# The residual's product, the last copy and the store at the tail of a one-token decode layer

## The chip, the cores and the metric

The kernel runs on one core of one Trainium2 chip. Its time is the device time of one execution in microseconds; lower is better. The kernel before took 191.78 us, the median of 3 runs (191.37 to 191.93).

## The reference, cut to what matters

One token of width 512 goes through an attention block with a cached history of 16384 positions (32 query heads, 8 key and value heads of width 128), and then through a block of four matrices. The two residual sums at the end are what the change touches.

```python
x = A_x
h = x + _A_ref(_layernorm(x), A_k_cache, A_v_cache, A_wq, A_wo)
h2 = h + _B_ref(_layernorm(h), B_w1, B_w2, B_w3, B_w4)

def _B_ref(x, w1, w2, w3, w4):
    h = _gelu(_layernorm(x) @ w1)
    ...                      # four blocks of h, each shifted along the token axis
    x1 = x + hs              # one token only: every shift leaves zeros, so hs is 0
    h2 = _gelu(_layernorm(x1) @ w3) @ w4
    return x1 + h2
```

With one token the shifted part is zero, so the kernel never loads `w1` and `w2`. What is left after the attention is: normalise h twice, multiply by `w3` (512 to 1792), gelu, multiply by `w4` (1792 to 512), and add h and the once normalised h. The output is 512 numbers in bf16, 1024 bytes.

## The kernel before, in words

All large loads go through SP's queue, and their transfers run one after the other: the query matrix, then keys and values of four pairs of heads, then `wo`, `w3` and `w4`. VectorE transposes the keys, TensorE makes scores and weighted values, and ScalarE takes the exponentials. After the last pair follows the tail: the attention's output through `wo` (line 728), the sum with x and its statistics (lines 482 to 533), the product with `w3` (line 746), gelu on ScalarE (line 758), a transpose on VectorE (line 762), the product with `w4` (line 772), a copy out of PSUM (line 777) and the store (line 778).

The product with `w4` takes 1792 rows as 14 parts of 128, m = 0 to 13. `W4` cuts its load into four pieces: parts 0 to 4, 5 to 9, 10 to 12, and 13. A part's matmuls wait for its piece. For each m there are four matmuls, o = 0 to 3: each has 32 columns of weights (`hcol[:, m, :]`, the same column 32 times) and writes 32 partitions of one PSUM bank, so that partitions 32o to 32o + 31 hold the o-th quarter of the result, 32 times over.

The residual h plus normalised h is `xsum`, [128, 128] in fp32, made by GpSimd (line 755); it has the same four quarters on its partitions. Ahead of part 10 one fp32 matmul with the identity (line 768, 128 columns of weights, the full array) adds it into the same bank. Then comes a mark, `pe(None)`: there the program sets a branch that is never taken back. VectorE has such a mark, `dve(None)`, behind its last transpose; before the change nothing of the kernel follows it there.

The order of work on each engine is the order in which the program calls `P.op`. Waits come from its lists of who wrote and read each key. One rule bears on the change: a `bank` key makes an operation wait for the latest operation of every other engine that named the same bank, whether it reads or writes:

```python
for k in bank:
    for e, o in self.users.get(k, {}).items():
        if e != eng:
            need(o, False)
```

Of the kernel before, what the change touches and what calls it, by code (L numbers as in the profile page):

```python
# [7 lines left out]
BF16 = mybir.dt.bfloat16  # L8
I32 = mybir.dt.int32
ALU = mybir.AluOpType  # L10
ACTF = mybir.ActivationFunctionType
# [316 lines left out]
NHC = FM // 128  # L328
WO = ((0, 12), (12, 24), (24, 30), (30, 32))
VP = 2  # L330
W3 = ((0, 2), (2, 3), (3, 4))
W4 = ((0, 5), (5, 10), (10, 13), (13, 14))
PAIRS = HKV // 2
RPARTS = 9
QPAD = 4 * 7
# [6 lines left out]
def bass_sequential_preLN__gqa_block_cached__mixer_s_mlp__decode_kernel(  # L342
# [13 lines left out]
    with ExitStack() as ctx:  # L356
        sb = lambda name, shape, dt: ctx.enter_context(nc.sbuf_tensor(name, shape, dt))
        ps = lambda name, shape, dt: ctx.enter_context(nc.psum_tensor(name, shape, dt))
        P = Program(nc, ctx)
# [15 lines left out]
        ident_f = sb("ident_f", [128, 128], FP32)  # L375
# [12 lines left out]
        xn = sb("xn", [128, NCH], BF16)  # L388
        qcol = sb("qcol", [128, 4, PAIRS * REP, 32], FP32)
        qb = sb("qb", [128, 4, PAIRS, QW], BF16)  # L390
        qn = sb("qn", [128, 4, QW], BF16)
# [19 lines left out]
        xsum = sb("xsum", [128, 128], FP32)  # L411
        hg = sb("hg", [128, FQ], BF16)
        hT = sb("hT", [128, NCH, 32], FP32)
        hcol = sb("hcol", [128, NHC, 32], BF16)
        fin = sb("fin", [128, 128], BF16)
        kb_all = sb("kb", [128, 256 * DH], BF16)
        kb = [kb_all[:, i * 128 * DH:(i + 1) * 128 * DH] for i in range(2)]
        vb = sb("vb", [128, 256 * DH], BF16)
# [3 lines left out]
        w4_sb = kb[1][:, NCH * FM:2 * NCH * FM].rearrange("p (m c) -> p m c", m=NHC)  # L422
# [6 lines left out]
        m_ps, n_ps = mn_ps[:, 0:256], mn_ps[:, 256:512]  # L429


        def load(name, dst, src, key, by="SP", also=()):
            P.op(by, lambda e: e.dma_start(dst, src), w=[key, *also], dma=name)

        def pair_rows(src, j):
            return src[0, 2 * j:2 * j + 2].rearrange("g (u t) d -> (g u) (t d)", u=64)
# [6 lines left out]
        def load_values(j):  # L443
            n = 256 // VP * DH
            if j < PAIRS - 1:
                load("v", vb[:, :], pair_rows(A_v_cache, j), ("v", 0),
# [11 lines left out]
        def dve(fn, r=(), w=(), bank=()):  # L458
            return P.op("DVE", fn, r, w, bank)

        def act(fn, r=(), w=(), bank=()):
            return P.op("ACT", fn, r, w, bank)
# [4 lines left out]
        def pe(fn, r=(), w=(), bank=(), also=()):  # L467

            return P.op("PE", fn, r, w, bank, also=also)

        def piece(cuts, m):
            return [lo <= m < hi for lo, hi in cuts].index(True)
# [48 lines left out]
        def inverse_root(i, n, by):  # L521
# [7 lines left out]
            for k in range(3):  # L529
# [22 lines left out]
            r=["ident", "x4"], w=["quarter"])  # L552
        pe(lambda e: e.matmul(O_ps[0][:, 0:128], quarter[:, :, :].rearrange("p q u -> p (q u)"), x4[:, :],
                              start=True, stop=True), r=["quarter"], w=[("O", 0)], bank=[("O", 0)])
# [9 lines left out]
            r=["ident_f"], w=["row32"])  # L564
        dve(lambda e: e.tensor_reduce(maskdd[:, :], ident_f[:, :].rearrange("p (n d) -> p d n", d=4), AX.X, ALU.add),
            r=["ident_f"], w=["maskdd"])
# [6 lines left out]
        for z, m, key, mk in ((zo, rowgh, "zo", "rowgh"), (zd, maskgh, "zd", "maskgh")):  # L573
# [5 lines left out]
            r=["hT", (("st", 0), 0), (("st", 0), 6)] + [("v", x) for x in range(VP)], w=["xn"])  # L579
# [3 lines left out]
        for i, key in enumerate(keys):  # L583
            P.part("query", i)
            for k in range(NCH):
                pe(lambda e, k=k: e.matmul(row[:, bass.ds(P.b, 512)], copies(xn[:, k:k + 1], 128),  # L586
                                           wq_k[:, k, bass.ds(P.c, REP * DH)], start=(k == 0), stop=(k == NCH - 1)),
                   r=["xn"], also=[("v", x) for x in range(VP)], w=["n" if key == "mn" else key], bank=[key])
        P.part()
        for g in range(2):  # L590
            half = banks[64 * g:64 * g + 64, PAIRS * g:PAIRS * g + PAIRS, :].rearrange("p j c -> p (j c)")
            for b in range(2):
                dve(lambda e, g=g, b=b, half=half: e.transpose(  # L593
                    qcol[64 * g:64 * g + 64, 2 * b:2 * b + 2, :, :].rearrange("p e m u -> p (e m u)"),
                    half.rearrange("p (m b i e) -> p b e m i", b=2, i=32, e=2)[:, b, :, :, :]),
                    r=["n" if x == "mn" else x for x in keys[PAIRS * g:PAIRS * g + PAIRS]], w=["qcol"],
                    bank=keys[PAIRS * g:PAIRS * g + PAIRS])
        for a in range(4):
# [118 lines left out]
        w4_in = B_w4.rearrange("(p m) c -> p m c", p=128)  # L717
        for n, (lo, hi) in enumerate(W4):
            load(f"w4{n}", w4_sb[:, lo:hi, :], w4_in[:, lo:hi, :], ("r", 1, len(W3) + n))
# [3 lines left out]
            r=["o_m"], w=["o_f"])  # L723
        dve(lambda e: e.tensor_copy(o_b[:, :], o_f[:, :]), r=["o_f", ("r", 0, 0)], w=["o_b"])  # L724

        for r_ in range(32):
            q = r_ % 4
            pe(lambda e, r_=r_, q=q: e.matmul(O_ps[0][32 * q:32 * q + 32, :], copies(o_b[:, r_:r_ + 1], 32),  # L728
                                              wo_sb[:, r_ * D:(r_ + 1) * D], start=(r_ < 4), stop=(r_ >= 28)),
               r=["o_b"] + [("r", 0, n) for n in (piece(WO, r_),) if n], w=[("O", 0)], bank=[("O", 0)])  # L730
        h_ps, hkey = banks[:, 6, :], "spare0"
        dve(lambda e: e.tensor_copy(osum[:, :], O_ps[0][:, :]), r=[("O", 0)], w=["osum"], bank=[("O", 0)])
        for q in range(4):
            pe(lambda e, q=q: e.matmul(h_ps[32 * q:32 * q + 32, 0:128], copies(row32[:, 0:1], 32),
                                       osum[:, q * 128:(q + 1) * 128], start=True, stop=True),
               r=["osum", "row32"], w=[hkey], bank=[hkey])
# [4 lines left out]
            r=["hT", (S, 0)] + [("r", 1, 0)], w=["hc"])  # L741


        for k in range(NCH):
            for q in range(4):
                pe(lambda e, k=k, q=q: e.matmul(s_ps[32 * q:32 * q + 32, 0, 0:FQ], hc[:, k, :],
                                                w3_sb[:, k, q * FQ:(q + 1) * FQ], start=(k == 0), stop=(k == NCH - 1)),
                   r=["hc"] + [("r", 1, n) for n in (piece(W3, k),) if n], w=[("s", 0)], bank=[("s", 0)])
# [5 lines left out]
            r=["hr", (S, 0), (S, 6)], w=["xs"])  # L754
# [9 lines left out]
                hg[:, :].rearrange("p (i m) -> p m i", m=NHC)[:, lo:hi, :]), r=[("hg", n)], w=[("hcol", n)])  # L764
        dve(None)
        for m in range(NHC):
            if m == W4[-2][0]:
                pe(lambda e: e.matmul(n_ps[:, 0:128], ident_f[:, :], xsum[:, :], start=False, stop=False,
                                      skip_group_check=True), r=["ident_f", "xsum"], w=["n"], bank=["mn"])
                pe(None)  # L770
            for o in range(4):
                pe(lambda e, m=m, o=o: e.matmul(  # L772
                    n_ps[32 * o:32 * o + 32, 0:128], hcol[:, m, :], w4_sb[:, m, o * 128:(o + 1) * 128],
                    start=(m == 0), stop=(m == NHC - 1),
                    skip_group_check=True),
                   r=[("hcol", 2 * m // NHC), ("r", 1, len(W3) + piece(W4, m))], w=["n"], bank=["mn"])
        act(lambda e: e.activation(fin[:, :], n_ps[:, 0:128], ACTF.Identity), r=["n"], w=["fin"], bank=["mn"])
        P.op("SP", lambda e: e.dma_start(out[0, 0:1, :].rearrange("o (q j) -> (o q) j", q=4), fin[0:128:32, :]),
             r=["fin"], w=["out"], dma="out")
        P.op("SP", lambda e: e.nop(), r=["out"])  # L780
        P.emit()

# [29 lines left out]
```

## Time and profile before

| | us |
|---|---|
| median of the runs shown | 191.78 |
| the three runs | 191.93, 191.78, 191.37 |
| profiled execution: span from first to last instruction | 190.4 |
| the median less that span | 1.4 |
| TensorE busy in the span | 118.6 |
| VectorE busy in the span | 118.2 |
| ScalarE busy in the span | 9.3 |

Of the profiled execution the page gives the span alone. Its own time is the span and what lies ahead of and behind it; taken at the median, that is 190.4 and 1.4. The transfers moved 79.20 MB at a mean of 416 GB/s over the span. A timeline row gives the start, the length, the engine, the line, the operation, the tiles and shapes, how many instructions are merged in it, and in brackets the idle time before it with what ended it. PE is TensorE's matmuls, PEld its weight loads, DVE VectorE, ACT ScalarE, POOL GpSimd and SPq the queue of SP.

### The profile page before, as it was taken

How to read it: one execution, taken by the hardware profiler on the slowest of the kernel's cores; microseconds unless marked ns; L12 is line 12 of the kernel's file. 1: busy time of each engine (PE TensorE's matmuls, PEld its weight loads, DVE VectorE, ACT ScalarE, POOL GpSimd, SP SyncE). 2: the span in 40 equal slices, each digit the busy share in tenths (PEclk: the TensorE clock that was granted, in tenths of full speed). 3: DMA queues.
4: the chain of work that ended last, by engine and by line, in shares of the span. 5: the costliest groups of instructions: out<-in, count | busy, mean ns of one | idle time of the engine just before them, and what ended most of it. 6: DMA issues, size and time to landing. Idle time of an engine off the chain costs nothing.

```text
span 190.4 us, 2182 instructions
## 1 busy us (share of the span) xinstructions
PE 118.6 (62%) x695; PEld 46.1 (24%) x695; DVE 118.2 (62%) x155; ACT 9.3 (5%) x16; POOL 7.3 (4%) x16
## 2 busy tenths in 40 slices
PE   0119709996195599940944989508449995294644
PEld 0103203442031143310311433203113332031212
DVE  6740799995504989845049989350479895504370
ACT  3000000000200000011000000020000000500020
POOL 7100000000000000000000000000000000000060
PEclk9999985899958579995585899975979999758855
DMA  6999999999999999997999999979999999989991
GB/s 227 434 441 441 441 441 441 441 441 441 413 441 406 420 523 441 441 441 330 441 441 441 523 441 413 441 324 420 413 441 441 441 441 441 441 367 421 409 411 51
DMA packets 3619, 79.20 MB, mean 416 GB/s; under 512 B 416, under 2 KB 544, under 8 KB 1568
## 3 DMA queue, kind: packets, MB, share of 16 engines
q1 hardware_dynamic: 3608, 79.17, 97.2%
q8 instruction: 1, 0.02, 0.0%
q14 instruction: 2, 0.02, 0.0%
q10 hardware_dynamic: 8, 0.00, 0.0%
HBM read 79.17 MB, written 0.00 MB: 416 GB/s over the span
## 4 chain that ended last, share of the span: by engine, by line
PE 39%; DMA 37%; DVE 16%; issue 4%; ACT 2%; ACTq 0%; SPq 0%; DVEq 0%
DMA kb<-in_A_k_cache_dram 31%; PE banks L626 22%; PE banks L662 6%; DMA vb<-in_A_wq_dram 6%; DVE kt L609 6%; PE banks L586 5%; DVE pt L651 3%; PE banks L728 2%; DVE mx L636 1%; ACT p_sb L647 1%; PE banks L620 1%; DVE od L681 1%; PE banks L772 1%; DVE qcol L593 1%; PE banks L639 1%
## 5 line engine op out<-in xcount | busy, mean ns | idle before, releaser
L609 DVE STREAM_TRANSPOSE kt<-kb 128x2048 int32<-128x2048 int32 (+1 forms) x37 | 71.3, 1987 | 4.3 <-DMA kb<-in_A_k_cache_dram 2.8
L626 PE MATMUL banks<-kt,qn 128*128 x256 | 68.7, 414 | 0.5
L626 PEld LDWEIGHTS banks<-kt,qn 128*128 x256 | 26.2, 102 | 41.4 <-issue 24.6
L662 PE MATMUL banks<-vb,pt 128*32 128x512 bf16 x256 | 24.4, 565 | 2.8 <-POOLq L448 2.8
L678 DVE TENSOR_SCALAR od<-banks,rowc 128x128 f32<-128x128 f32 x4 | 1.4, 350 | 26.3 <-PE banks L662 26.3
L620 PE MATMUL banks<-qn 128*128 128x512 bf16 x8 | 4.0, 495 | 17.3 <-DVE kt L609 17.1
L651 DVE STREAM_TRANSPOSE pt<-p_sb 64x1024 bf16<-64x1024 bf16 x8 | 9.9, 1239 | 5.4 <-ACT p_sb L647 5.3
L662 PEld LDWEIGHTS banks<-vb,pt 128*32 128x32 bf16 x256 | 9.0, 136 | 16.4 <-issue 12.4
L586 PE MATMUL banks<-vb,xn 128*128 x32 | 8.9, 446 | 6.1 <-DVE xn L577 6.1
L669 PE MATMUL banks<-acc,zd 128*32 128x1 f32 x8 | 1.1, 202 | 17.7 <-DVE pt L651 17.7
L647 ACT ACTIVATE p_sb<-banks,bias 128x1024 bf16<-128x1024 f32 x4 | 4.5, 1113 | 155.4 <-DVE nmh L643 155.4
L636 DVE TENSOR_REDUCE mx<-banks 128x1 f32<-128x1024 f32 x4 | 4.9, 1224 | 8.1 <-PE banks L626 8.1
L593 DVE STREAM_TRANSPOSE qcol<-banks 64x1024 f32<-64x1024 f32 x4 | 4.8, 1226 | 6.9 <-PE banks L586 6.9
L528 POOL TENSOR_SCALAR st<-st 128x1 f32<-128x1 f32 x1 | 0.2, 241 | 176.1 <-DVE st L513 176.1
L586 PEld LDWEIGHTS banks<-vb,xn 128*128 128x128 bf16 x32 | 3.6, 112 | 11.0 <-issue 8.5
L639 PE MATMUL banks<-mxd,mean 128*128 128x128 f32 x8 | 2.0, 326 | 6.6 <-DVE mxd L637 6.6
L620 PEld LDWEIGHTS banks<-qn 128*128 128x128 bf16 x8 | 0.8, 100 | 20.2 <-issue 20.0
L684 PE MATMUL banks<-od,zo 128*32 128x128 f32 x8 | 1.6, 285 | 6.5 <-DVE od L681 6.5
L669 PEld LDWEIGHTS banks<-acc,zd 128*32 128x32 f32 x8 | 0.7, 140 | 18.4 <-DVE pt L651 18.4
L681 DVE SCALAR_TENSOR_TENSOR od<-banks,rowc,od 128x128 f32<-128x128 f32 x12 | 4.2, 351 | 0.4
L550 DVE CAST ident<-ident_f 4x4 bf16<-4x4 f32 x1 | 3.8, 3848 | 0.6 <-POOL ident_f L545 0.6
L728 PE MATMUL banks<-kb,o_b 128*32 128x512 bf16 x32 | 3.5, 583 | 1.1 <-DVE o_b L724 1.1
(78 smaller groups left out, 44.6 us busy)
## 6 DMA issues: line engine op xcount, KB each, us to landing
kb<-in_A_k_cache_dram SPq DMA_DIRECT2D x8, 4096.0 KB, 29.7
vb<-in_A_v_cache_dram SPq DMA_DIRECT2D x2, 4096.0 KB, 29.2
vb<-in_A_wq_dram SPq DMA_DIRECT2D x1, 4096.0 KB, 12.3
kb<-in_A_wo_dram SPq DMA_DIRECT2D x2, 1536.0 KB, 25.4
kb<-in_B_w_dram SPq DMA_DIRECT2D x2, 640.0 KB, 25.4
kb<-in_B_w_dram SPq DMA_DIRECT2D x1, 896.0 KB, 22.4
kb<-in_B_w_dram SPq DMA_DIRECT2D x2, 448.0 KB, 23.4
kb<-in_A_wo_dram SPq DMA_DIRECT2D x1, 768.0 KB, 28.5
```

What stands on the lines that cost most here:

```text
L586: pe(lambda e, k=k: e.matmul(row[:, bass.ds(P.b, 512)], copies(xn[:, k:k + 1], 128), wq_k[:, k, bass.ds(P.c, REP * DH)], start=(k == 0), s ...
L593: dve(lambda e, g=g, b=b, half=half: e.transpose(qcol[64 * g:64 * g + 64, 2 * b:2 * b + 2, :, :].rearrange("p e m u -> p (e m u)"), half.r ...
L609: P.op("DVE", lambda e, view=view: e.transpose(view(kt), view(kb[y])), r=[("r", y, i) for i in range(RPARTS)], w=[("kt", t + i) for i in r ...
L620: pe(lambda e: e.matmul(row[:, bass.ds(P.y, 512)], copies(none, 128), copies(none, 512), start=True, stop=False, skip_group_check=True), r ...
L626: pe(lambda e, n=n: e.matmul(row[:, bass.ds(P.y, 512)], qn[:, n, bass.ds(P.q, 128)], key_piece(P.k, n), start=False, stop=(n == 3), skip_g ...
L636: dve(lambda e: e.tensor_reduce(mx[:, :], s_all, AX.X, ALU.max), r=[("s", 0), ("s", 1)], w=["mx"], **both)
L639: pe(lambda e: e.matmul(m_ps[:, 0:128], mean4[:, :], mxd[:, :], start=True, stop=True), r=["mxd", "mean4"], w=["m"], bank=["mn"])
L647: act(lambda e: e.activation(p_sb[:, :], s_all, ACTF.Exp, bias=bias[:, 0:1], scale=float(SCALE), accum_out=acc[:, :]), r=[("s", 0), ("s", ...
L651: dve(lambda e, g=g: e.transpose(pt[64 * g:64 * g + 64, :, :, g, :], p_sb[64 * g:64 * g + 64, :]), r=["p"], w=["pt"])
L662: pe(lambda e, l=l, ct=ct, ch=ch: e.matmul(O_ps[0][32 * ct:32 * ct + 32, :], pt[:, l, ch, :, :].rearrange("p g u -> p (g u)"), tiles[:, l ...
L681: dve(lambda e, block=block, c=c: e.scalar_tensor_tensor(od[:, :], block, rowc[:, c:c + 1], od[:, :], ALU.mult, ALU.add), r=[key, "rowc", ...
L728: pe(lambda e, r_=r_, q=q: e.matmul(O_ps[0][32 * q:32 * q + 32, :], copies(o_b[:, r_:r_ + 1], 32), wo_sb[:, r_ * D:(r_ + 1) * D], start=(r ...
```

## The change

Three edits in the last 20 lines:

- The residual's product moves from ahead of part 10 to ahead of part 7 (`NHC // 2`, the first part of the second half), and becomes four matmuls of 32 columns of weights instead of one of 128. The mark `pe(None)` stays ahead of part 10.
- The four quarters are written to the partitions in the order 0, 2, 1, 3 (`BLOCK`). So partition 31 and partition 32, which are neighbours, hold quarters 0 and 2 of the result in the lower half of the bank, and the upper half of the bank holds quarters 1 and 3. ScalarE copies partitions 0 to 63 into the first 128 columns of `fin`, VectorE copies partitions 64 to 127 into the second 128. Partition 31 of `fin` is then the first half of the output, partition 32 the second.
- The store takes these two rows of 512 bytes instead of four rows of 256 bytes, and waits for both copies.

```diff
+BLOCK = (0, 2, 1, 3)
...
-        fin = sb("fin", [128, 128], BF16)
+        fin = sb("fin", [64, 256], BF16)
...
         for m in range(NHC):
+            if m == NHC // 2:
+                for o in range(4):
+                    pe(lambda e, o=o: e.matmul(
+                        n_ps[32 * o:32 * o + 32, 0:128], ident_f[:, 32 * BLOCK[o]:32 * BLOCK[o] + 32], xsum[:, :],
+                        start=False, stop=False, skip_group_check=True),
+                       r=["ident_f", "xsum"], w=["n"], bank=["mn"])
             if m == W4[-2][0]:
-                pe(lambda e: e.matmul(n_ps[:, 0:128], ident_f[:, :], xsum[:, :], start=False, stop=False,
-                                      skip_group_check=True), r=["ident_f", "xsum"], w=["n"], bank=["mn"])
                 pe(None)
             for o in range(4):
                 pe(lambda e, m=m, o=o: e.matmul(
-                    n_ps[32 * o:32 * o + 32, 0:128], hcol[:, m, :], w4_sb[:, m, o * 128:(o + 1) * 128],
+                    n_ps[32 * o:32 * o + 32, 0:128], hcol[:, m, :], w4_sb[:, m, BLOCK[o] * 128:(BLOCK[o] + 1) * 128],
...
-        act(lambda e: e.activation(fin[:, :], n_ps[:, 0:128], ACTF.Identity), r=["n"], w=["fin"], bank=["mn"])
-        P.op("SP", lambda e: e.dma_start(out[0, 0:1, :].rearrange("o (q j) -> (o q) j", q=4), fin[0:128:32, :]),
-             r=["fin"], w=["out"], dma="out")
+        act(lambda e: e.activation(fin[:, 0:128], n_ps[0:64, 0:128], ACTF.Identity),
+            r=["n"], w=[("fin", 0)], bank=["mn"])
+        dve(lambda e: e.tensor_copy(fin[:, 128:256], n_ps[64:128, 0:128]), r=["n"], w=[("fin", 1)], bank=["mn"])
+        P.op("SP", lambda e: e.dma_start(out[0, 0:1, :].rearrange("o (q j) -> (o q) j", q=2), fin[31:33, :]),
+             r=[("fin", 0), ("fin", 1)], w=["out"], dma="out")
```

## The prediction

> **What bounds the kernel now.** I read the page first, then the tail alone: its timeline, its chain of waits, its stretches by window, and the groups by line. The page:
>
> ```profile
> span 190.4 us, 2182 instructions
> PEclk9999985899958579995585899975979999758855
> DMA  6999999999999999997999999979999999989991
> ```
>
> The transfers are busy in every slice but the first and the last, so until the last weights have landed the kernel runs at their pace. Nothing in the change touches that. What counts is the last slices: there the transfers stop, and TensorE's granted clock is half.
>
> ```profile
> 184.41 1.04 DVE L762 STREAM_TRANSPOSE hcol<-hg 128x224 bf16<-128x224 bf16 x2 [0.61 <-ACT hg L758]
> 185.22 0.45 POOL L755 TENSOR_TENSOR xsum<-hr,xs 128x128 f32<-128x128 f32 x1
> 185.76 0.46 PEld L772 LDWEIGHTS banks<-kb,hcol 128*32 128x32 bf16 x20 [0.26 <-DMA kb<-in_B_w_dram]
> 186.16 0.33 PE L772 MATMUL banks<-kb,hcol 128*32 128x128 bf16 x4
> 186.41 0.50 PEld L768 LDWEIGHTS banks<-xsum,ident_f 128*128 128x128 f32 x2 [0.20 <-issue]
> 186.42 0.80 PE L768 MATMUL banks<-xsum,ident_f 128*128 128x128 f32 x2
> 187.14 0.62 PE L772 MATMUL banks<-kb,hcol 128*32 128x128 bf16 x16
> 187.81 0.28 ACT L777 ACTIVATE fin<-banks 128x128 bf16<-128x128 f32 x1 [3.08 <-PE banks L772]
> 188.12 0.63 SPq L778 DMA_DIRECT2D out_dram<-fin  x1
> ```
>
> This is the tail's timeline. Part 5 of the last matrix starts at 185.76, when its piece has landed; part 9's four matmuls are the row at 186.16. The residual's product then holds TensorE from 186.41, and part 10 starts at 187.14. After the last matmul come a copy of 0.28 and the store's issue. The store's wait is in the view of who waits for whom on SP's queue:
>
> ```profile
> SPq L780 <- DMA out_dram<-fin: 1.6, 1, 1.6
> ```
>
> So the store takes 0.63 of issue and 1.6 of waiting, from 188.12 to the span's end at 190.4: longer than TensorE takes from part 5 to its last matmul, 185.76 to 187.76. Three terms can move: when TensorE ends, how long the copies take, and the store.
>
> **The product moved.** First, how early could part 10 start at all? Its piece is the 384 KB load, part 13's the 128 KB one:
>
> ```profile
> 165.63 3.16 SPq L433 DMA_DIRECT2D kb<-in_B_w_dram  x1
> 168.83 0.43 SPq L433 DMA_DIRECT2D kb<-in_B_w_dram  x1
> kb<-in_B_w_dram SPq DMA_DIRECT2D x1, 384.0 KB, 21.1
> kb<-in_B_w_dram SPq DMA_DIRECT2D x1, 128.0 KB, 18.2
> ```
>
> Issue plus time to landing: 165.63 + 21.1 = 186.73 and 168.83 + 18.2 = 187.03. A wait hands over in about 0.03 (worked out below), so part 10 can't start before 186.76. Now it starts at 187.14: the product's place costs 0.38 at most, and that is the cap on what moving it brings. Part 13 comes three groups of 0.10 later, at 187.06 or after; its own gate is 187.06 too, so it is hardly held.
>
> Second, what does the product cost in its new place and form? A group of four bf16 matmuls is 0.10 long: the 20 matmuls from part 5 to 9 run from 185.76 until part 9 starts at 186.16, four groups on, 0.40. The new product is four fp32 matmuls of 32 columns, each in two passes; line 734 has just that form:
>
> ```profile
> 179.32 0.43 PE L734 MATMUL banks<-osum,row 128*32 128x128 f32 x8 [0.79 <-DVE osum L732]
> L734 PE MATMUL banks<-osum,row x8: 272/284/297, 179.3 to 179.5; 128*32 128x128 f32 x8
> 178.00:180.00 2.00, 0.95 (x16) 0.25 (x10) 0.88 (x2) 0.00 (x0) 0.00 (x0) 1.00 0.98 403
> 186.00:187.00 1.00, 1.00 (x22) 0.72 (x11) 0.00 (x0) 0.00 (x0) 0.00 (x0) 0.50 0.26 91
> 186.79 0.42 PE L768 MATMUL banks<-xsum,ident_f 128*128 128x128 f32 x1
> ```
>
> Eight matmuls take 0.43, and the last ones 0.27 of it, so the second passes start some 0.15 after the first, or 0.13 if the four are issued in 0.02. That is at full clock (in the two rows by window the third figure from the end, the granted clock, is 1.00 there and 0.50 in the tail). At half clock I take twice 0.13 for each pass, 0.52 for the product. The bounds: nothing doubled, 0.26; and the pass of the old product, which runs at the tail's clock but loads 128 columns, 186.79 less 186.42 = 0.37, twice 0.74. Of the three I take 0.52: right form, clock corrected.
>
> Part 7 is reached at 185.76 plus two groups, 185.96. GpSimd's `xsum` ends at 185.22 + 0.45 = 185.67 and the second transpose at 184.41 + 1.04 = 185.45, so the moved wait costs nothing by 0.29; were `xsum` later than that, parts 7 to 13 would all queue behind it. Then five groups (0.52) and the product (0.52) put part 10 at 186.80, just behind its gate. Gain: 187.14 - 186.80 = **-0.34** (-0.12 with 0.74, -0.38 at the gate). What goes with the old form, and is in these numbers: 186.41 is 0.25 after part 9's start where a next group comes after 0.10, so 0.15 of idling ahead of the full-array product; the new form has the tile shape of its neighbours. The 12 added TensorE instructions (8 loads and 8 matmuls for 2 and 2) stand ahead of the mark and no transfer is moved. The copies can only start after part 13, so the whole 0.34 reaches them.
>
> **The copies.** The code says halves, but not at once. Both copies name the bank `mn`, and by the bank rule VectorE's copy, called second, waits for ScalarE's. So the path is ScalarE, then VectorE, then SP. ScalarE's half has 64 partitions instead of 128 but the same 128 columns: 0.28 kept. VectorE's copy is not in the trace; near rows, all reading PSUM:
>
> ```profile
> L494 DVE COPY st<-banks x2: 159/160/160, 7.6 to 180.9; 128x2 f32<-128x2 f32 x2
> 178.57 0.69 DVE L732 COPY osum<-banks 128x512 f32<-128x512 f32 x1 [3.61 <-PE banks L728]
> L678 DVE TENSOR_SCALAR od<-banks,rowc 128x128 f32<-128x128 f32 x4 | 1.4, 350 | 26.3 <-PE banks L662 26.3
> 183.89 0.85 ACT L758 ACTIVATE hg<-banks,st 128x224 bf16<-128x224 f32 x2 [2.37 <-DVE st L533]
> L758 ACT ACTIVATE hg<-banks,st 128x224 bf16<-128x224 f32 x2 | 0.8, 485 | 2.4 <-DVE st L533 2.4
> ```
>
> Between 2 columns (0.16) and 512 (0.69) a copy of 128 falls at 0.16 + 126/510 x 0.53 = 0.29. Ends: 0.16, and 0.35 for line 678's operation of the same shape. The handover ScalarE to VectorE is 183.89 + 0.49 = 184.38 to 184.41, 0.03. **+0.32** (+0.19 to +0.38). It can't be below nothing: it is added behind a copy that keeps its columns. Nothing is queued behind this wait on VectorE; SP's store waits for it. SP's extra wait for ScalarE is over by then.
>
> Here the Trainium skill speaks against the wait: PSUM — Partial Sum Buffer, section PSUM bank collisions raise a hardware error, says two engines may use one bank at the same time in different quadrants of 32 partitions, and that guarding by whole banks is only the simple version. The halves are different quadrants, so by it the wait is not needed, and side by side the copies would give about +0.01 here instead of +0.32. No row shows two engines reading one bank at once, and the program's rule decides.
>
> **The store.** Nearest row: the store itself, 2.26 for four rows of 256 bytes. What of it can two rows save? The packets and the wait:
>
> ```profile
> 186.40:186.60 0.20, 0.20 (x5) 0.19 (x2) 0.00 (x0) 0.00 (x0) 0.00 (x0) 0.50 0.21 77
> 186.60:186.80 0.20, 0.20 (x2) 0.20 (x2) 0.00 (x0) 0.00 (x0) 0.00 (x0) 0.50 0.00 0
> 189.30:189.45 0.15, 0.00 (x0) 0.00 (x0) 0.00 (x0) 0.00 (x0) 0.00 (x0) 0.50 0.05 7
> 189.45:190.30 0.85, 0.00 (x0) 0.00 (x0) 0.00 (x0) 0.00 (x0) 0.00 (x0) 0.50 0.00 0
> 0.71 0.55 ACTq L433 DMA_DIRECT2D x<-in_A_x_dram  x1
> ```
>
> The store's packets move within 189.30 to 189.45, and the span ends at 190.4: 0.95 in which only a receipt is awaited. The last weights' packets end by 186.60 and their landing is 187.03: 0.43. If the store's receipt fell to that, it would save 0.5; that is the lower end. The upper end is +0.1, the 0.08 by which two issues of four such rows differ (0.63 and 0.55). I take **-0.15**, under a third of the way from the store's own row to the lower end, because the wait is for the slowest row and there are two instead of four.
>
> **Sum.** -0.34 + 0.32 - 0.15 = -0.17. The profiled execution is its span of 190.4 and the 1.4 around it, the median of the runs: 191.78 - 0.17 = 191.61. Between runs of before lie 0.56 (0.3%), and 0.3% is about what a measurement of this kernel can tell from no change: 0.57 here. The forecast is within it.
>
> **The rivals.** *The receipt falls by all of 0.5:* 191.78 - 0.34 + 0.32 - 0.5 = 191.26, and with the ends of the other terms 191.09. For it: 0.95 against 0.43. Against: one lands in device memory and one on chip, and only the row length differs in the change. DMA: Bandwidth & Descriptors of the Trainium skill says for it, in Specifications, that below 512 B the engine reads, modifies and writes; its section Anatomy of one DMA says against it that the fixed part is mostly the receipt and scales with nothing. No row shows a 512-byte store.
>
> *The copy eats more than the product gives:* if the four-part product takes 0.74, TensorE gains 0.12; with a copy of 0.35 and no saving in the store it is 191.78 - 0.12 + 0.38 = 192.04, slower, though inside 0.3%. The point is a product longer than about 0.5. For it: the half clock, and no row of the four-part form at that clock.
>
> *Code that isn't there yet:* slower by more than 0.3%.
>
> ```profile
> q8 instruction: 1, 0.02, 0.0%
> 187.00:187.10 0.10, 0.10 (x1) 0.00 (x0) 0.00 (x0) 0.00 (x0) 0.00 (x0) 0.50 0.65 164
> ```
>
> One instruction packet is fetched on q8; with no weights left, the window's 0.65 of 16 engines for 0.10 is this packet, 1.04 of one engine: code coming from 187.0 to 188.1. If the 12 added instructions push TensorE's last ones into it, the last parts wait until 188.1 instead of running from 187.1: +1.0, less the other terms, 192.6. It decides only if the boundary lies within those 12; now the last parts run while it is on its way.
>
> **How the numbers follow.** Forecast, the product's gain spent on the copy: 0.64. Receipt down by about 0.5: 0.22, most of it past 0.3% only with the other ends or a good run. Copy over product: 0.06, inside 0.3%. Late code: 0.08. Past -0.3% I put 0.19, the receipt's case and little else; past +0.3% 0.09; within 0.72. The range goes from 191.05 (the receipt's case with the ends) to 192.15 (192.04 and the upper end of the store): only late code and the rare best case are outside.
>
> **What would show it.** Right: line 768's successor as eight short matmuls near 185.97, no gap of 0.2 around it, part 10 at about 186.8; ScalarE's copy at 187.47 and VectorE's not beside it but behind, with ScalarE as its releaser; the store's issue at 188.1 as before. Wrong: part 10 at 187.0 or later (the product); both copies starting together (the wait); a wait for the store near 1.1 (the receipt); TensorE idle behind the mark with its weights landed (the code).

## The result, and the profile after

The changed kernel takes 192.84 us (median of 6 runs, 192.71 to 193.20). The kernel before took 191.86 on the same chips (median of 6, 191.37 to 192.23). The ratio is 1.0047, with a 95% interval of 1.0031 to 1.0063: slower by about 0.98 us. The forecast was 191.61 with a range up to 192.15, so it was wrong, on the slow side. In the experiments below one execution each of e1, e3 and e11 was disturbed (above 194 us, 2 us or more above all others of its kernel) and is left out of every figure.

The page of the profile says the opposite, and that is the lesson of this case:

```profile
span 189.6 us, 2197 instructions
```

The span got shorter, 189.6 against 190.4, while the time got longer. The profiled execution took 192.94, so 3.3 us lie ahead of or behind the span, where before it was 1.4 (at the median). The runs agree: each gives its own time and span, and the time less the span is 3.31 to 3.50 in all 6 runs after, and 1.27 to 1.50 in all 60 runs of the kernel before that were made beside the experiments below.

The rows of the timeline that matter in the tail after (start, length, engine, line, operation, tiles and shapes, count, idle time before and its releaser):

```profile
185.52 0.94 PE L777 MATMUL banks<-kb,hcol 128*32 128x128 bf16 x28 [1.79 <-DVE hcol L763]
185.71 0.45 POOL L756 TENSOR_TENSOR xsum<-hr,xs 128x128 f32<-128x128 f32 x1
186.25 0.64 PE L770 MATMUL banks<-xsum,ident_f 128*32 128x128 f32 x8
186.67 0.96 PE L777 MATMUL banks<-kb,hcol 128*32 128x128 bf16 x28
187.69 0.27 ACT L782 ACTIVATE fin<-banks 64x128 bf16<-64x128 f32 x1 [2.47 <-PE banks L777]
188.06 0.29 DVE L784 CAST fin<-banks 64x128 bf16<-64x128 f32 x1 [2.12 <-ACT fin L782]
188.43 0.33 SPq L785 DMA_DIRECT2D out_dram<-fin  x1
```

And the store's wait, in the view of what SP's queue waited for:

```profile
SPq L787 <- DMA out_dram<-fin: 0.8, 1, 0.8
```

The order that was forecast for the inside of the span is there: eight short matmuls of the product with no gap before them, the last weights' matmuls right behind (first seven parts from 185.52, last seven from 186.67), ScalarE's copy, VectorE's behind it with ScalarE as its releaser. The times are later than forecast, since the tail itself starts at 185.52 instead of 185.04. The store is much better than forecast: its issue takes 0.33 instead of 0.63 and its wait 0.8 instead of 1.6. So the loss is not in the span. What stands behind the span? VectorE's last instruction used to be the second transpose, which ended at 185.45. Now it is line 784, which ends at 188.35. The trace keeps a few records after the span that the views do not list: packets of code on queue q14, and the marks that the engines raise when they reach the end of the program (updates of one semaphore). Those of the two profiled executions:

| us from the span's start | before | after |
|---|---|---|
| VectorE's last instruction ends | 185.45 | 188.35 |
| VectorE's next code packet (8192 bytes) | 186.57 | 189.40 |
| VectorE's end mark | 188.58 | 191.40 |
| store landed | 190.36 | 189.58 |
| SP's end mark | 190.51 | 191.42 |

Which end mark and which code packets are VectorE's is inferred: they are those that move with VectorE's last instruction. The mark stands 3.1 us behind that instruction in both, and a packet of code is fetched in between. A second packet follows 2.4 us behind the first, at 189.02 before and at 191.84 after. Before, all of this was over while the store was still on its way. After, VectorE's mark stands 1.8 us behind the store's landing, and SP's mark 0.02 behind VectorE's: 191.42 less 190.51 is 0.91, next to the 0.98 measured. The packet itself can be seen in the windows (the last two figures are the share of the 16 DMA engines and GB/s; the store's own two packets are the first row):

```profile
189.15:189.25 0.10, 0.00 (x0) 0.00 (x0) 0.00 (x0) 0.00 (x0) 0.00 (x0) 0.50 0.05 10
189.40:189.50 0.10, 0.00 (x0) 0.00 (x0) 0.00 (x0) 0.00 (x0) 0.00 (x0) 0.50 0.28 82
```

82 GB/s over 0.10 us are 8.2 KB, and no instruction of the kernel moves data there.

### The profile page after: what moved, and what is told of

Same layout as the page of the kernel before. It is cut to its first block, busy times and chain, and to the rows that moved or that the text cites. A ratio compares the mean times of both kernels' runs of the same rounds, so it can differ in the third digit from the quotient of the medians.

```text
span 189.6 us, 2197 instructions
## 1 busy us (share of the span) xinstructions
PE 115.8 (61%) x701; PEld 45.7 (24%) x701; DVE 118.6 (63%) x156; ACT 9.3 (5%) x16; POOL 7.3 (4%) x16
## 4 chain that ended last, share of the span: by engine, by line
DMA 77%; DVE 13%; PE 7%; issue 1%; SPq 1%; ACT 0%; DVEq 0%; ACTq 0%
DMA kb<-in_A_k_cache_dram 61%; DMA kb<-in_A_wo_dram 15%; DVE kt L610 10%; PE banks L627 4%; SPq L434 1%; PE banks L777 1%; DVE st L532 0%; DVE osum L733 0%; PE banks L621 0%; PE banks L493 0%; DVE hcol L763 0%; ACT hg L759 0%; PE banks L735 0%; PE banks L770 0%; PE banks L729 0%
## 5 line engine op out<-in xcount | busy, mean ns | idle before, releaser
L627 PE MATMUL banks<-kt,qn 128*128 x256 | 69.8, 422 | 0.2
L627 PEld LDWEIGHTS banks<-kt,qn 128*128 x256 | 26.7, 104 | 41.8 <-issue 24.9
L663 PE MATMUL banks<-vb,pt 128*32 128x512 bf16 x256 | 22.7, 532 | 2.8 <-POOLq L449 2.8
L587 PE MATMUL banks<-vb,xn 128*128 x32 | 8.4, 429 | 6.4 <-DVE xn L578 6.4
L663 PEld LDWEIGHTS banks<-vb,pt 128*32 128x32 bf16 x256 | 8.5, 128 | 15.2 <-issue 10.3
L729 PE MATMUL banks<-kb,o_b 128*32 128x512 bf16 x32 | 2.7, 384 | 2.4 <-DMA kb<-in_A_wo_dram 1.3
```

The lines of the kernel that those rows point to most:

```text
L627: pe(lambda e, n=n: e.matmul(row[:, bass.ds(P.y, 512)], qn[:, n, bass.ds(P.q, 128)], key_piece(P.k, n), start=False, stop=(n == 3), skip_g ...
L663: pe(lambda e, l=l, ct=ct, ch=ch: e.matmul(O_ps[0][32 * ct:32 * ct + 32, :], pt[:, l, ch, :, :].rearrange("p g u -> p (g u)"), tiles[:, l ...
```

## The experiments

Each was timed beside the kernel before on the same chip, and the ratio is to that kernel.

**Is it VectorE being last?** My theory: the time is lost because VectorE's last instruction comes late, wherever it is and whatever it does. The rivals: it is lost elsewhere in the changed tail, in the longer chain of copies, or in the longer code of TensorE.

*e1_scalar_halves* is the changed kernel with both copies on ScalarE:

```diff
-        dve(lambda e: e.tensor_copy(fin[:, 128:256], n_ps[64:128, 0:128]), r=["n"], w=[("fin", 1)], bank=["mn"])
+        act(lambda e: e.activation(fin[:, 128:256], n_ps[64:128, 0:128], ACTF.Identity),
+            r=["n"], w=[("fin", 1)], bank=["mn"])
```

> The changed kernel with both halves copied by ScalarE, so that VectorE has nothing to do behind its mark. Theory, VectorE's end code: VectorE fetches more code about 1.05 us behind its last instruction and reports its end about 3.05 us behind it, and a last instruction at 188.35 makes this the last thing of the execution. Here its last instruction is the transpose again, so the end is the store's: issue near 188.2, landing near 189.4, time about 1.4 above the span, 190.8 to 191.1 us (0.8 to 1.0 under the kernel before). Rival, the longer chain of copies: the two copies still stand one behind the other, so only the hand-over is saved and the time stays near the changed kernel's, 192.5 to 192.8 us.

Measured: 191.15, ratio 0.9953 [0.9935, 0.9971]. The timeline of the copies and the store:

```profile
187.79 0.27 ACT L782 ACTIVATE fin<-banks 64x128 bf16<-64x128 f32 x1 [2.47 <-PE banks L777]
188.08 0.27 ACT L784 ACTIVATE fin<-banks 64x128 bf16<-64x128 f32 x1
188.38 0.33 SPq L786 DMA_DIRECT2D out_dram<-fin  x1
```

The copies are as long and the store starts at nearly the same time (188.38 against 188.43). Inside the span nothing is changed (189.5 against 189.6), and the time falls by 1.7 us, time less span by 1.75 (1.63 against 3.38, medians of the runs). So neither rival holds: the chain of two copies and TensorE's code are those of the changed kernel. The change is faster than the kernel before as soon as its second copy is taken off VectorE.

*e4_late_vector_op* is the other way round: the kernel before, with one element copied by VectorE behind ScalarE's last copy. Nobody waits for it.

```diff
+        dve(lambda e: e.tensor_copy(scr[0:1, 2:3], fin[0:1, 0:1]), r=["fin"], w=["late"])
```

> The kernel before and one VectorE copy of a single element, behind ScalarE's last copy, for which nobody waits. Theory, VectorE's end code: its last instruction ends near 188.3 instead of 185.45, and the time rises by 0.8 to 0.95 us to 192.6 to 192.8 us, with the span unchanged at 190.4. Rival, the longer chain: nothing waits for it, so 191.8 us, no change.

Measured: 193.21, ratio 1.0066 [1.0051, 1.0080].

```profile
188.73 0.63 SPq L778 DMA_DIRECT2D out_dram<-fin  x1
188.73 0.14 DVE L780 CAST scr<-fin 1x1 f32<-1x1 bf16 x1 [2.48 <-ACT fin L777]
```

An instruction of 0.14 us, off every path of the kernel's data, costs 1.3 us. Time less span is 3.39 as in the changed kernel, though its TensorE code is that of before. That settles it: the late VectorE instruction is the cause, and the rivals fall. The size was missed, 192.6 to 192.8 having been expected: in the profiled execution VectorE's end mark comes 3.78 behind its last instruction, not 3.05, and why is open.

*e2_halves_alone* is the kernel before with the copy split over ScalarE and VectorE, four rows stored as before, product not moved:

```diff
-        act(lambda e: e.activation(fin[:, :], n_ps[:, 0:128], ACTF.Identity), r=["n"], w=["fin"], bank=["mn"])
+        act(lambda e: e.activation(fin[0:64, :], n_ps[0:64, 0:128], ACTF.Identity),
+            r=["n"], w=[("fin", 0)], bank=["mn"])
+        dve(lambda e: e.tensor_copy(fin[64:128, :], n_ps[64:128, 0:128]), r=["n"], w=[("fin", 1)], bank=["mn"])
...
```

> The kernel before with the copy alone changed: partitions 0 to 63 by ScalarE, 64 to 127 by VectorE, store of four rows of 256 bytes as before. Theory, VectorE's end code: VectorE's last instruction ends near 188.45 and its end comes 3.05 later, 1.0 us behind the end of the kernel before: 192.8 us. Rival, the longer chain alone: +0.35 for the second copy, 192.2 us.

Measured: 193.19, ratio 1.0069 [1.0053, 1.0085]. Half of the change alone loses more than the whole: the late end is there (its mark stands at 191.58), and neither the moved product nor the shorter store is there to give something back. It is also 0.4 above the 192.8 that was expected for the median; the profiled execution took 192.85.

**What starts VectorE's last code packet?** The kernel has a mark on VectorE, `dve(None)`, a branch never taken back, ahead of the last copy. Theory A: the packet belongs to the end of the program and comes when VectorE gets there. Theory B: the mark holds it back, and without the mark it would have come earlier. (The mark is two things, a branch hint near the start of VectorE's program and the branch itself.)

*e10_early_mark*: the changed kernel with `dve(None)` moved ahead of the attention's last reduction, at about 174 us.

```diff
+        dve(None)
         dve(lambda e: e.tensor_reduce(o_f[:, :], o_m[:, :, :].rearrange("p d r -> p r d"), AX.X, ALU.add),
...
-        dve(None)
         for m in range(NHC):
```

> The changed kernel with VectorE's mark ahead of the tail's first VectorE instruction, near 174 us instead of 185, where VectorE waits for nothing of the last matrices. If the branch starts the fetch of the code behind it, that code is there long before the copy ends, and the time is that of the store, 190.9 to 191.3 us. If the fetch starts only when VectorE reaches the end of its instructions, 192.8 us, as the changed kernel.

Measured: 192.80, ratio 1.0039 [1.0024, 1.0054]; the packet comes at 189.26, 1.04 behind VectorE's last instruction. So passing the branch does not start the fetch; by its time, reaching the end does.

*e6_no_vector_mark*: the changed kernel without the mark.

```diff
     def _vector(self):
         eng = self.nc.vector
-        rv = eng.alloc_register("never")
-        hint = eng.mark_branch_hint_location()
-        eng.reg_mov(rv, 0)
...
-        eng.br_lt(rv, 0, "body", "ve_on").branch_hint(hint)
-        self.nc.switch_bb("ve_on", parent=None)
```

> The changed kernel without VectorE's mark: neither the hint at the start nor the branch; the copy stands behind the transposes in one run of instructions. Theory A, the code behind VectorE's last instruction is fetched only when VectorE gets there, mark or not: 192.8 us, as the changed kernel. Theory B, the mark holds the fetch back: without it the code comes earlier, and the store ends last, 190.9 to 191.3 us.

Measured: 191.61, ratio 0.9974 [0.9963, 0.9985]. The packet is fetched at 53.35 us, in the middle of the stream of keys and values, and VectorE's end mark comes 0.90 behind its last instruction instead of 3.05. So B holds, in the end: without the mark the code is there early. The gain is smaller than what was expected under B because the tail begins later:

```profile
186.31 0.94 PE L772 MATMUL banks<-kb,hcol 128*32 128x128 bf16 x28 [1.76 <-DVE hcol L758]
188.90 0.29 DVE L779 CAST fin<-banks 64x128 bf16<-64x128 f32 x1 [2.17 <-ACT fin L777]
189.27 0.33 SPq L780 DMA_DIRECT2D out_dram<-fin  x1
```

It starts at 186.31 where the one after starts at 185.52. The median span of its runs is 190.05, against 189.45 after.

*e12_before_no_mark*: the kernel before, without that mark (the same five lines taken out).

> The kernel before without VectorE's mark. Its VectorE ends early, so nothing is to be gained at the end. Theory: the code that the mark held back is fetched in the middle of the stream of weights instead, near 53 us as in the changed kernel without the mark, and the stream on that engine ends later by about the time of the packet, 0.3 us: 191.8 to 192.5 us, no change or slower. Rival, the fetch in the stream costs nothing: the ratio is 1.000.

Measured: 191.93, ratio 0.9990 [0.9976, 1.0003]; no difference that can be told. The store waits 1.0 instead of 1.6, a gain of 0.6, but the last weights' packets end at 187.13 instead of 186.55, a loss of 0.6. It is so in all three kernels without the mark: these packets end at 187.13 to 187.49 there (e6, e11, e12), and at 186.46 to 186.85 in the eleven others. In the medians of the runs the spans of e6 and e11 (190.05 and 189.70) are longer by 0.65 than those of e10 and e7 (189.40 and 189.05), which are the same but for the mark or its place. So taking the mark out gains at the end and costs about 0.6 in the stream that bounds the kernel. That the one packet at 52.10 does it is not shown: it takes 0.31 us, half of that loss.

**Does VectorE's copy have to wait for ScalarE's?** *e7_halves_together*: the changed kernel, with the bank's key left out of VectorE's copy. It still waits for TensorE.

```diff
-        dve(lambda e: e.tensor_copy(fin[:, 128:256], n_ps[64:128, 0:128]), r=["n"], w=[("fin", 1)], bank=["mn"])
+        dve(lambda e: e.tensor_copy(fin[:, 128:256], n_ps[64:128, 0:128]), r=["n"], w=[("fin", 1)])
```

> The changed kernel without the bank key on VectorE's copy, so that the two halves are copied at the same time. Theory, VectorE's end code: VectorE's last instruction ends near 188.0 instead of 188.35, so all that follows it comes 0.37 us earlier: 192.4 to 192.6 us, still above the kernel before. Rival, the wait between the copies is the cause: without it the kernel is under the one before, 191.4 us or less.

Measured: 192.67, ratio 1.0032 [1.0018, 1.0046].

```profile
187.30 0.27 ACT L782 ACTIVATE fin<-banks 64x128 bf16<-64x128 f32 x1 [2.67 <-PE banks L777]
187.30 0.29 DVE L784 CAST fin<-banks 64x128 bf16<-64x128 f32 x1 [1.96 <-PE banks L777]
187.67 0.33 SPq L785 DMA_DIRECT2D out_dram<-fin  x1
```

Both copies start at 187.30, and neither is longer than in turn (0.27 and 0.29). From ScalarE's start to the store's issue it is 0.37 instead of 0.74. So the wait was not needed, which agrees with the section of the Trainium skill that the prediction cited (PSUM — Partial Sum Buffer, PSUM bank collisions raise a hardware error). The kernel is still slower than before, as was expected, because the copy that now ends at 187.60 is still VectorE's last instruction and late: time less span is 3.51.

*e11_together_no_mark*: the edits of e6 and e7 in one kernel.

> The changed kernel without VectorE's mark and without the bank key on VectorE's copy: both halves are copied at the same time and the code behind them is there. Against the changed kernel without the mark (191.6 us) the store is issued 0.37 us earlier and ends last: 191.2 to 191.3 us. If VectorE's end code were still what ends last, it would stay at 191.6.

Measured: 191.25, ratio 0.9956 [0.9936, 0.9976], time less span 1.56. With both edits the change gains, with VectorE's copy in it.

**What made the store shorter, and why was it so long before?** *e9_rows_of_256*: e1 with the quarters in their old order, so that each of the two partitions holds two pieces of 256 bytes that lie apart in the output.

```diff
-BLOCK = (0, 2, 1, 3)
+BLOCK = (0, 1, 2, 3)
...
-        P.op("SP", lambda e: e.dma_start(out[0, 0:1, :].rearrange("o (q j) -> (o q) j", q=2), fin[31:33, :]),
+        P.op("SP", lambda e: e.dma_start(out[0, 0:1, :].rearrange("o (h q j) -> (o q) h j", h=2, q=2),
+                                         fin[31:33, :].rearrange("p (h j) -> p h j", h=2)),
```

> The kernel with both halves copied by ScalarE, and the store of the same two partitions as four pieces of 256 bytes (quarters in their old order, so that a partition's two pieces lie apart in the output). Theory, the number of rows that are spread over the engines sets the store: two partitions, so 0.33 of issue and 0.8 of waiting as with rows of 512 bytes, 191.1 to 191.3 us. Rival, the length of a row sets it: 256 bytes bring back the store of the kernel before, a wait of 1.0 to 1.9 us and an end 0.5 to 1.1 us later, 191.7 to 192.3 us.

Measured: 190.94, ratio 0.9940 [0.9924, 0.9956], the lowest of all versions here, though its interval overlaps those of e1, e8, e11 and e13. The kernel before took 192.16 beside it.

```profile
188.26 0.32 SPq L786 DMA_DIRECT2D out_dram<-fin  x1
SPq L789 <- DMA out_dram<-fin: 0.9, 1, 0.9
```

An issue of 0.32 and a wait of 0.9 for four pieces of 256 bytes, 0.33 and 0.8 for two of 512. The Trainium skill (DMA: Bandwidth & Descriptors, Specifications) says that below 512 B the engine reads, modifies and writes; no cost of that shows in a store of 1 KB. It is the number of partitions that counts, two against four, and not the length of the pieces.

*e13_store_alone*: the kernel before, with two copies on ScalarE and e9's store; product not moved.

```diff
...
-        act(lambda e: e.activation(fin[:, :], n_ps[:, 0:128], ACTF.Identity), r=["n"], w=["fin"], bank=["mn"])
+        for h in range(2):
+            act(lambda e, h=h: e.activation(fin[:, 128 * h:128 * h + 128], n_ps[64 * h:64 * h + 64, 0:128],
+                                            ACTF.Identity), r=["n"], w=[("fin", h)], bank=["mn"])
...
```

> The kernel before with the end alone changed: ScalarE copies both halves, and the store takes four pieces of 256 bytes from two partitions; the residual's product where it was, nothing for VectorE behind its mark. Theory: +0.3 for the second copy, and 1.0 to 1.3 less for the store (a store from two partitions took 1.2 us in the earlier runs, one from four 1.6 to 2.5), together 0.5 to 1.0 us under the kernel before: 190.9 to 191.5 us. If the gain of the kernels with ScalarE's halves came from the moved product and not from the store, it is above the kernel before by 0.3.

Measured: 191.18, ratio 0.9949 [0.9929, 0.9969].

```profile
188.11 0.57 ACT L778 ACTIVATE fin<-banks 64x128 bf16<-64x128 f32 x2 [2.89 <-PE banks L772]
188.70 0.32 SPq L780 DMA_DIRECT2D out_dram<-fin  x1
SPq L783 <- DMA out_dram<-fin: 0.8, 1, 0.8
```

A second ScalarE copy costs 0.28 and the store gives back 1.1. Nearly the whole gain of e1 and e9 is here, without the product.

*e8_vector_op_at_xsum* was meant as a control for e4: the same one-element copy, but behind `xsum`, at about 186, where VectorE's end is still early.

```diff
+        dve(lambda e: e.tensor_copy(scr[0:1, 2:3], xsum[0:1, 0:1]), r=["xsum"], w=["late"])
```

> The kernel before and one VectorE copy of a single element behind GpSimd's xsum, ready near 185.7 us, so that VectorE's last instruction ends near 185.9 instead of 185.45. Theory: VectorE's end comes 3.05 later, near 189.0, and the end of the store at 190.4 hides it: 191.8 to 192.1 us, no change, where the same operation behind ScalarE's last copy cost 1.3 us. Rival, any instruction behind the mark costs: 1.0 us or more above the kernel before.

Measured: 191.26, ratio 0.9954 [0.9937, 0.9971]. As a control it holds: an instruction behind the mark costs nothing as long as VectorE's end is early. But it was a miss too: I expected no change, and the kernel before gets faster by 0.68 us from an instruction that does nothing for it.

```profile
185.94 0.14 DVE L780 COPY scr<-xsum 1x1 f32<-1x1 f32 x1 [0.25 <-POOL xsum L755]
188.16 0.63 SPq L778 DMA_DIRECT2D out_dram<-fin  x1
SPq L781 <- DMA out_dram<-fin: 1.0, 1, 1.0
```

The store is issued as before (188.16 against 188.12), but waits 1.0 instead of 1.6. The records of single packets say why. Before, VectorE's two code packets near the end come at 186.57 and 189.02, and the second meets the store's: three rows land at 189.72 to 189.73, the fourth at 190.36. The second one shows in the windows of before, where no instruction moves data, as 55 GB/s over 0.15 us, again 8.2 KB:

```profile
188.90:189.05 0.15, 0.00 (x0) 0.00 (x0) 0.00 (x0) 0.00 (x0) 0.00 (x0) 0.50 0.14 55
```

In e8 VectorE ends 0.63 later (186.08), its packets come at 187.32 and 189.88, the second after the store's rows have landed at 189.74 to 189.81, all four together. In e3 below, the last row's packet starts at 189.768, where a code packet ends at 189.771, and one row lands at 190.67; e2 has the same picture (189.969 and 189.972, the row at 190.92).

So the kernel before had a store with one row stuck behind VectorE's code. In e4 and e12, where no code packet is under way when the store's packets move, the wait is 1.0 too. That the row and the code share a DMA engine is inferred, since the records do not name the engine: e13's two rows move while a code packet is under way, and land together. How the delay comes about is open: in e3 three rows land 0.37 to 0.38 behind their packets, and the late one 0.88 behind its own.

**The product.** *e3_product_alone*: the kernel before with the product moved and cut in four, and nothing else.

```diff
+            if m == NHC // 2:
+                for o in range(4):
+                    pe(lambda e, o=o: e.matmul(
+                        n_ps[32 * o:32 * o + 32, 0:128], ident_f[:, 32 * o:32 * o + 32], xsum[:, :],
+                        start=False, stop=False, skip_group_check=True),
+                       r=["ident_f", "xsum"], w=["n"], bank=["mn"])
             if m == W4[-2][0]:
-                pe(lambda e: e.matmul(n_ps[:, 0:128], ident_f[:, :], xsum[:, :], start=False, stop=False,
-                                      skip_group_check=True), r=["ident_f", "xsum"], w=["n"], bank=["mn"])
```

> The kernel before with the residual's product alone moved ahead of part 7 as four matmuls; copy and store as before. Both theories: part 10 starts 0.1 to 0.36 us earlier and all behind it too; the time falls by as much, 191.4 to 191.75 us. If it falls by nothing, the product was never on the path that ends last.

Measured: 191.96, ratio 0.9996 [0.9976, 1.0016] over 11 runs. Also a miss: no gain. (Two of the 11 took 190.73 and 190.84, the next one 191.80; no trace shows what differed in them.)

```profile
185.64 0.94 PE L776 MATMUL banks<-kb,hcol 128*32 128x128 bf16 x28 [1.75 <-DVE hcol L762]
187.86 0.28 ACT L781 ACTIVATE fin<-banks 128x128 bf16<-128x128 f32 x1 [2.53 <-PE banks L776]
SPq L784 <- DMA out_dram<-fin: 1.9, 1, 1.9
```

TensorE does take less: from the first matmul with `w4` to the copy 187.86 less 185.64 = 2.22, against 187.81 less 185.04 = 2.77 before. But in this execution it started 0.60 later, the store's late row waited for the code packet 0.3 longer, and in the median of the runs the span is 190.4 against 190.5, the time less the span 1.55 against 1.32. That last 0.2 stands in the kernels with the moved product whose VectorE ends early or has no mark (e1 1.63, e3 1.55, e6 1.56, e9 1.58, e11 1.56), and not in those without it (e8 1.36, e12 1.34, e13 1.34). In the records it stands behind SP's end mark: from there to the last mark of all 1.50 to 1.67 pass in the profiled executions with the moved product, and 1.31 to 1.43 in those without it. Its cause is open: the product's new form has 12 more instructions on TensorE, and no run here varied their number. Inside the span the moved product does show, 189.4 for e9 against 189.8 for e13, which has the same store without it. What it is worth in the end can't be told from nothing: e9 stands at 0.9940 [0.9924, 0.9956], e13 at 0.9949 [0.9929, 0.9969].

The end marks behind all this, from the records of the profiled executions that bear on it (us from the span's start):

| kernel | VectorE's last instruction ends | its end mark | SP's end mark | time | time less the later mark |
|---|---|---|---|---|---|
| after | 188.35 | 191.40 | 191.42 | 192.94 | 1.5 |
| e2 | 188.51 | 191.58 | 191.60 | 192.85 | 1.2 |
| e4 | 188.88 | 192.65 | 192.68 | 193.93 | 1.3 |
| e7 | 187.60 | 190.86 | 190.88 | 192.31 | 1.4 |
| e1 | 186.04 | 188.96 | 189.65 | 191.15 | 1.5 |
| e6 | 189.19 | 190.10 | 190.54 | 192.04 | 1.5 |
| e9 | 185.53 | 188.67 | 189.60 | 191.09 | 1.5 |
| e13 | 185.94 | 188.93 | 190.00 | 191.20 | 1.2 |

The time is the later of two ends, VectorE's program and the store, and 1.2 to 1.5 more. In the first four SP's mark stands 0.02 behind VectorE's; in the last four VectorE's is earlier, and SP's stands 0.15 behind the store's landing.

## Why the prediction was wrong

**The step that failed** is the sum's frame: "The profiled execution is its span of 190.4 and the 1.4 around it", carried over as if the 1.4 were a constant, and with it the sentence on VectorE's copy, "Nothing is queued behind this wait on VectorE". Something was queued there: the end of VectorE's program, 3.05 us from its last instruction to its end mark, with a code packet in it. It had been hidden behind TensorE's last parts and the store; the change moved its start by 2.9 us and took the cover away. The 1.4 became 3.3. The prediction asked what is queued behind the wait, and looked for instructions of the kernel alone.

**Code that isn't there yet** had the right mechanism in the wrong place: I looked for it on TensorE, inside the span, with the packet on q8. TensorE shows no idle time behind its mark. The page of before listed code packets for a second queue as well:

```profile
q14 instruction: 2, 0.02, 0.0%
```

By their times they were VectorE's. After, the page counts one, at 189.40, 0.2 ahead of the span's end. The rival was priced at 192.6 and given 0.08. The Trainium skill (Runtime: NRT & Kernel Launch, Instruction fetch mechanics) calls the cost of fetching the next block of code mostly hidden; the trace agrees for the kernel before, and not for the one after, where the last fetch and what follows it are 1.8 us longer than the store.

**The product moved**, -0.34: right in mechanism and near in size. Its length is 186.67 less 186.25 = 0.42, where I took 0.52, and e7, which starts 0.10 ahead of the kernel before and waits for part 5's piece as that does, goes from first matmul to copy in 2.36 where that took 2.77: -0.41. Part 10 at 187.0 or later was the prediction's sign of a failed product, and after it starts at 187.01; but that is the later start of the tail, and in e7 it starts at 186.63. What was wrong is that all of it reaches the end: e3 shows that it doesn't, with 0.3 lost to the store's late row and 0.2 behind the span.

**The copies**, +0.32: from ScalarE's start to the store's issue 0.74, against 0.31 before (187.81 to 188.12), so +0.43. VectorE's copy is 0.29 as interpolated. Mis-sized was the hand-over between engines: 0.10 from ScalarE's end to VectorE's start (187.96 to 188.06) and 0.08 from VectorE's end to SP, not 0.03. The row I took 0.03 from had VectorE's wait standing right ahead of the instruction; here the records show a separate wait of VectorE for ScalarE ahead of the copy, from 187.99 to 188.02.

**The store**, -0.15: from issue to the span's end 1.17 (188.43 to 189.6) against 2.26, so -1.09. This term was mis-sized by far, beyond its end of -0.5. Two things were behind it that no row I quoted could show. Two partitions rather than four halve the issue (0.33 for 0.63; I had only two issues of four rows to go by, 0.63 and 0.55). And of the 0.95 which I read as "only a receipt is awaited", 0.6 was one row behind VectorE's code packet (e8). With that gone the landing comes 0.39 after the packets start (189.19 to 189.58), near the 0.43 of a load that stood beside it. The rival on the receipt thus came near in size, 0.5 for 0.6, for the reason of neither section it named: not the row length (e9), and not a part that never changes. (The second, Anatomy of one DMA in DMA: Bandwidth & Descriptors of the Trainium skill, is written for transfers that GpSimd issues; this store is issued by SP.)

Put together, the span should have moved by -0.41 + 0.43 - 1.09 = -1.07. In the two profiled executions it moved by -0.8 only, since the tail began 0.48 later after (185.52 against 185.04); 0.19 of that took the place of a wait for part 5's piece (2.17 from first matmul to copy after, 2.36 in e7), and 0.29 was left. In the medians of the runs the span is 189.45 against 190.5 (the kernel before as timed beside e1 to e4), -1.05, and the time less the span 3.38 against 1.32, +2.06: together +1.0, the 0.98 that was measured. (The lower end of the range, 191.05, is also 0.04 below the 191.09 that the prediction's own terms give; nothing hangs on it.)

## What to carry to other kernels

Before you give an engine the last piece of work, ask when that engine's program would otherwise have ended: what it needs to finish may be hidden now and stand at the end then, here 3 us behind VectorE's last instruction. Compare the time less the span, and not the span alone; when it moves, the cause lies in what the page does not list. And when a short transfer at the end waits unusually long, look at the other queues' packets in that time, the instruction queues too, before you put it down to a fixed cost.

## What the runs showed of the hardware that was not expected

- VectorE's end (by the marks and packets that move with its last instruction): 8192 bytes of code are fetched 0.8 to 1.8 us behind its last instruction, and its end mark follows 2.8 to 3.8 us behind it (1.05 and 3.05 after), wherever the mark's branch is kept. ScalarE, with 17 counted instructions in e1 against VectorE's 155, marks its end 0.1 us behind its last.
- The mark, a branch hint and a branch that is never taken back, holds this fetch off until the engine has got to the end; which of the two does it was not tried. Without them a packet comes at 52 to 54 us (e6, e11, e12) and VectorE's mark 0.9 behind its last instruction in e6 and e11, but the last weights' packets end 0.3 to 1.0 later than in the kernels with the mark.
- Where a code packet ends just as a packet of the four-row store starts, one row lands 0.6 to 0.9 later than the others (before, e2, e3); where none is under way, all four land within 0.1 (e4, e8, e12).
- A store of 1 KB costs 0.63 to issue from four partitions and 0.32 or 0.33 from two, whether in pieces of 512 or 256 bytes.
